# Gated mix of cached attention and a GEGLU FFN, decode: products of 20 of 128 rows in PSUM, FFN weights loaded ahead of the last values, w_down's products spread over the last tile

## Chip, cores and metric

The kernel runs on one core of one Trainium2 chip. The metric is device time in microseconds of one execution, the median over runs. Besides, one execution was recorded by the hardware profiler; everything that is said of engines and queues comes from that recording.

## What is computed

One decode step for a batch of four: attention of 32 heads over a cache of 4096 keys and values, a GEGLU FFN on the same input, and a gate between them.

```python
# B=4, D=512, H=32, Sk=4096, Dh=128, F=1792, all float32
q = (x @ wq).reshape(B, 1, H, Dh).transpose(0, 2, 1, 3)
scores = einsum("bhqd,bhkd->bhqk", q, k_cache) * Dh**-0.5
p = softmax(scores)
a = einsum("bhqk,bhkd->bhqd", p, v_cache)          # -> (B, 1, H*Dh)
a = a @ wo
b = (gelu(x @ w_gate) * (x @ w_up)) @ w_down
g = sigmoid((x * gate_w).sum(-1))
out = g * a + (1 - g) * b
```

Keys and values are 268 MB each; everything else is 28 MB.

## The kernel before

The attention runs over 32 tiles. Tile i is four heads (HT) of one batch row b; four tiles make a group g. A head's 4096 positions lie on 32 partitions with 128 rows (R) of 128 numbers each, so that a tile of keys is 128 partitions by 16384 floats, 8.39 MB, and one of values the same.

All large data passes through three buffers of that size (`kv`), used in turn: wq, k0, v0, k1, v1, and so on, and at the end f (w_gate and w_up), d (w_down and the first 18 rows of wo) and w (the last 14 rows of wo, in five pieces). Every load is issued on SyncE's queue, in this order; `load_next` issues the next one. A load waits until the last reader of its buffer is done: k(i+2) waits for the products of v(i), v(i+1) for the sum over k(i).

The order on each engine is as the program writes it. For one tile:

- VectorE multiplies the keys in place by the query (`multiply`, L188), sums over each row of 128 (`add_up`, L191) into SC, and finds a head's maximum (L200 to L204).
- ScalarE takes the exponentials into PM (`weights`, L207).
- TensorE multiplies PM with the values (`values`, L225, 32 products of two passes) into one of two PSUM banks PO[i % 2]; ScalarE copies that out (L228), TensorE gathers it into G (L231). Within iteration i this is done for tile i-1, after `multiply(i)` in program order.
- After a group, `totals` (L215) and `quotients` (L233 to L242) divide by the sums into OT, and `spread` (L173) lays out the next group's queries in QB by way of the bank QP.

In the last tile `multiply` and `add_up` go in pieces of 32 rows (CH), and ScalarE sums the first 32 rows (`add_up_beside`, L195).

Then comes the end: `totals`, `values` and `quotients` for the last tile; OT is spread over 128 partitions (L, L274; products L278) into OW (times the gate, L281) and OX (L284); FFN's up products (L294), gelu and gate (L296 to L306) into hT; 14 products with w_down and 18 with wo's first rows into one bank (L313); its copy a_sb (L315) starts the sum in acc (L318), wo's last 14 rows are added (L323), and the result is copied and stored (L326, L327).

Of the kernel before, what the change touches and what calls it, by code (L numbers as in the profile page):

```python
# [9 lines left out]
F32 = mybir.dt.float32  # L10
AF = mybir.ActivationFunctionType
OP = mybir.AluOpType
AX = mybir.AxisListType
# [4 lines left out]
def tile_gated_mix(ctx: ExitStack, tc: tile.TileContext, x, kc, vc, wq, wo, w_gate, w_up, w_down, gate_w, out):  # L18
    nc = tc.nc
    P = 128  # L20
    B, H, S, D = kc.shape
    DM = x.shape[2]
    F = w_gate.shape[1]
    KC = DM // P
    HT = 4
    PH = P // HT
    R = S // PH
    TW = R * D
    NG = H // HT
# [8 lines left out]
    CH = 32  # L38
    BASE = 24576
    scale = 1.0 / math.sqrt(D)  # L40
    c_gelu = math.sqrt(2.0 / math.pi)
# [9 lines left out]
    SC = front.tile([P, R], F32)  # L51
    RS = front.tile([P, B, HT], F32)
    QX = front.tile([P, B, HT, PH], F32)
# [3 lines left out]
    back = ctx.enter_context(tc.tile_pool(name="back", bufs=1))  # L57
# [3 lines left out]
    T = {}  # L61
# [10 lines left out]
    LOADS = []  # L72

    def load_kv(kind, i):
        nc.sync.dma_start(place((kind, i)), heads(kc if kind == "k" else vc, i))
# [17 lines left out]

    for i in range(NT):
        LOADS.append(lambda i=i: load_kv("k", i))
        LOADS.append(lambda i=i: load_kv("v", i))
    LOADS += [load_ffn_up, load_down, load_last]
    LOADS = iter(LOADS)

    def load_next():  # L100
        f = next(LOADS, None)
        if f:
            f()
# [23 lines left out]
    xT_ps = ps.tile([P, KC, B], F32, name="sm", bufs=2)  # L127
    for c in range(KC):
        nc.tensor.transpose(xT_ps[:, c, :], x_sb[:, c::KC], ident[:B, :B])  # L129
    for c in range(KC):  # L130
# [8 lines left out]
    z_ps = ps.tile([P, B], F32, name="sm", bufs=2)  # L139
# [5 lines left out]
    nc.vector.reciprocal(gates[:, 0], ez)  # L145
    nc.vector.tensor_scalar(gates[:, 1], gates[:, 0], -1.0, 1.0, op0=OP.mult, op1=OP.add)

    PO = [ps.tile([P, RJ * D], F32, name=f"po{s}") for s in range(2)]
    QP = ps.tile([P, B * D], F32, name="q")
    HG = H // 4  # L150
    HB = HG // 2
    w = T["q"].rearrange("p (c n) -> p c n", c=KC)
# [18 lines left out]
    QB = back.tile([P, B, D], F32)  # L171

    def spread(g):  # L173
        t = QP.rearrange("p (b d) -> p b d", b=B)
# [6 lines left out]
    dump = QX[:, 0].rearrange("p h k -> p (h k)")  # L181

    def keys(i):
        return T["k", i].rearrange("p (r d) -> p r d", d=D)

    def multiply(i, r0, r1):
        k = keys(i)[:, r0:r1]
        nc.vector.tensor_tensor(k, k, QB[:, i % B, None, :].to_broadcast([P, r1 - r0, D]), op=OP.mult)  # L188

    def add_up(i, r0, r1):  # L190
        nc.vector.tensor_reduce(SC[:, r0:r1], keys(i)[:, r0:r1], axis=AX.X, op=OP.add)  # L191

    def add_up_beside(i, r0, r1):
        for r in range(r0, r1):
            nc.scalar.activation(dump, keys(i)[:, r, :], AF.Copy, accum_out=SC[:, r:r + 1])  # L195

    def weights(i):
        b = i % B
# [12 lines left out]
    TOT = {}  # L211

    def totals(g):
        TOT[g] = ps.tile([P, B, HT], F32, name="sm", bufs=2)
        nc.tensor.matmul(TOT[g].rearrange("p b h -> p (b h)"), ones, RS.rearrange("p b h -> p (b h)"),  # L215
                         start=True, stop=True)

    def values(i):
        g, b = divmod(i, B)
        po = PO[i % 2]  # L220
        p = PM.rearrange("p r h -> p (r h)")
        n = R // RJ
        for j in range(n):
            c = j % 4
            nc.tensor.matmul(po[32 * c:32 * c + M], p[:, j * M:(j + 1) * M],  # L225
                             T["v", i][:, j * RJ * D:(j + 1) * RJ * D], start=j < 4, stop=j >= n - 4)
        o = back.tile([P, RJ * D], F32, name="o")
        nc.scalar.activation(o, po, AF.Copy)  # L228
# [4 lines left out]
    def quotients(g):  # L233
# [4 lines left out]
        t = ps.tile([P, B, HT], F32, name="sm", bufs=2)  # L238
# [3 lines left out]
        nc.vector.tensor_tensor(OT[:, :, HT * g:HT * g + HT], t, ri, op=OP.mult)  # L242

    spread(0)
    for i in range(NT):
        g, b = divmod(i, B)
        last = i == NT - 1
        multiply(i, 0, CH if last else R)
        if i > 0:
            if b == 0:  # L250
                totals(g - 1)
            values(i - 1)
            load_next()
        if b == 0 and i > 0:
            quotients(g - 1)
        if b == B - 1 and not last:
            spread(g + 1)
        if last:
            add_up_beside(i, 0, CH)
            for r in range(CH, R, CH):  # L260
                multiply(i, r, r + CH)
                add_up(i, r, r + CH)
        else:
            add_up(i, 0, R)
        weights(i)
        load_next()
    load_next()
    totals(NG - 1)
# [7 lines left out]
    t = ps.tile([P, B, 32], F32, name="sm", bufs=2)  # L276
# [9 lines left out]
    f = T["f"]  # L286
    spare = f[:, 2 * KC * F:2 * KC * F + 4 * FG].rearrange("p (a n) -> p a n", n=FG)
    u0, u1, t1, t2 = (spare[:, a, :] for a in range(4))
    for s, u in enumerate((u0, u1)):
        up = PO[s][:, :FG]  # L290
        for c in range(KC):
            for j in range(4):
                n0 = (s * KC + c) * F + j * FG
                nc.tensor.matmul(up[32 * j:32 * j + 32], xT[:, c, :], f[:, n0:n0 + FG],  # L294
                                 start=c == 0, stop=c == KC - 1)
        nc.scalar.activation(u, up, AF.Copy)  # L296
    nc.vector.tensor_tensor(t1, u0, u0, op=OP.mult)
    nc.vector.tensor_scalar(t1, t1, 0.044715, 1.0, op0=OP.mult, op1=OP.add)
    nc.vector.tensor_tensor(t1, t1, u0, op=OP.mult)
    nc.scalar.activation(t2, t1, AF.Tanh, scale=c_gelu)  # L300
    nc.vector.scalar_tensor_tensor(t1, t2, 1.0, u0, op0=OP.add, op1=OP.mult)
    nc.vector.scalar_tensor_tensor(t2, t1, 0.5, u1, op0=OP.mult, op1=OP.mult)
    hs = u0.rearrange("p (i r) -> p i r", i=DR)
    nc.vector.transpose(hs, t2.rearrange("p (q i) -> p i q", i=DR))
    hT = back.tile([P, DR, B], F32, name="hT")
    nc.vector.tensor_tensor(hT, hs[:, :, ::8], gates[:, 1, None, :].to_broadcast([P, DR, B]), op=OP.mult)  # L306

    a = QP
    early = [(hT[:, i, :], T["d"][:, i * DM:(i + 1) * DM]) for i in range(DR)]
    early += [(OW[:, :, i], T["d"][:, (DR + i) * DM:(DR + i + 1) * DM]) for i in range(W1)]  # L310
    for n, (l, r) in enumerate(early):
        c = n % 4
        nc.tensor.matmul(a[32 * c:32 * c + B], l, r, start=n < 4, stop=n >= len(early) - 4)  # L313
# [3 lines left out]
    for c in range(4):  # L317
        nc.tensor.matmul(acc[32 * c:32 * c + 32], pick_b.rearrange("p b k -> p (b k)"),  # L318
                         a_sb[:, c * P:(c + 1) * P], start=True, stop=False)
    for i in range(W1, WR):  # L320
        for c in range(4):
            r0 = (i - W1) * DM + c * P
            nc.tensor.matmul(acc[32 * c:32 * c + 32], OX[:, i - W1].rearrange("p b k -> p (b k)"),  # L323
                             T["w"][:, r0:r0 + P], start=False, stop=i == WR - 1)
    res = back.tile([P, P], F32, name="res")
    nc.vector.tensor_copy(res, acc)  # L326
    nc.sync.dma_start(out.rearrange("b s (c n) -> c (b s) n", c=4), res[::8])  # L327
# [22 lines left out]
```

## Time and profile before

| | |
|---|---|
| median of 3 runs | 1337.32 us (1337.11 to 1337.6) |
| the profiled execution | 1336.9 us, span 1335.0 us |
| mean granted TensorE clock | 0.645 |
| VectorE busy | 1133.3 us, 85% |
| TensorE busy | 387.6 us, 29% |
| ScalarE busy | 119.8 us, 9% |
| read from HBM | 564.67 MB, 423 GB/s over the span |

A row of groups names line, engine, operation, the tiles written and read, the shape and the count; after the first bar stands the busy time and the mean of one in ns; after the second the idle time of the engine just before, and what ended it. A row of the timeline starts with its start and length in us. DMA issues on SyncE's queue are shown as SPq.

### The profile page before, as it was taken

The page shows a single profiled execution, that of the slowest core. Times are in us where ns is not written, and L with a number is a line of the kernel's source. Part 1 is how long each engine was busy: PE and PEld are TensorE (multiplying, and loading weights), DVE is VectorE, ACT ScalarE, POOL GpSimd, SP SyncE. Part 2 cuts the span into 40 slices and gives each one's busy share as a digit, 9 for nine tenths or more (in the row PEclk, how much of TensorE's full clock was granted, in tenths as well). Part 3 has the DMA queues.
Part 4 walks back from the last instruction along what each step waited for, and adds up shares of the span by engine and source line. Part 5 has one row for each costly group of instructions (what it writes and reads, how often), then busy time and mean ns, then how long its engine had stood idle before and what let it go on. Part 6 is the DMA issues. An engine that isn't in the chain of part 4 may idle for free.

```text
span 1335.0 us, 6193 instructions
## 1 busy us (share of the span) xinstructions
PE 387.6 (29%) x2590; PEld 100.4 (8%) x2590; DVE 1133.3 (85%) x221; ACT 119.8 (9%) x408; POOL 0.7 (0%) x6
## 2 busy tenths in 40 slices
PE   2133212333321333321233232122333212323237
PEld 0000000000000001000010000000010000100002
DVE  1788889888889988888998898998888889888851
ACT  0000010001100010000000010000100000000130
POOL 0000000000000000000000000000000000000000
PEclk9566556666556666655666665566666556666658
DMA  9999999999999999999999999999999999999995
GB/s 409 440 438 410 440 426 431 430 434 416 425 434 428 434 423 414 434 430 430 429 432 429 430 423 436 423 432 432 424 438 428 427 432 436 432 420 419 434 426 219
DMA packets 10719, 565.07 MB, mean 423 GB/s; under 512 B 1196, under 2 KB 1212, under 8 KB 1604
## 3 DMA queue, kind: packets, MB, share of 16 engines
q1 hardware_dynamic: 10692, 564.69, 98.6%
q8 instruction: 20, 0.33, 0.1%
q14 instruction: 7, 0.06, 0.0%
HBM read 564.67 MB, written 0.01 MB: 423 GB/s over the span
## 4 chain that ended last, share of the span: by engine, by line
DVE 44%; DMA 38%; PE 14%; ACT 3%; issue 1%; DVEq 0%; SPq 0%; ACTq 0%
DMA kv<-in_A_k_cache 38%; DVE SC L191 22%; DVE kv L188 21%; PE po L225 12%; ACT PM L207 3%; PE q L313 1%; PE po L294 1%; DVE m L200 0%; DVE mt L202 0%; DVE nm L204 0%; PE g L323 0%; DVE OT L242 0%; DVE ri L235 0%; ACT o L228 0%; PE g L231 0%
## 5 line engine op out<-in xcount | busy, mean ns | idle before, releaser
L188 DVE TENSOR_TENSOR kv<-kv,QB 128x16384 f32<-128x16384 f32 (+1 forms) x35 | 551.6, 15761 | 122.0 <-DMA kv<-in_A_k_cache 122.0
L191 DVE TENSOR_REDUCE SC<-kv 128x128 f32<-128x16384 f32 (+1 forms) x34 | 547.0, 16088 | 2.6
L225 PE MATMUL po<-kv,PM 128*16 128x512 f32 x2048 | 298.6, 749 | 668.2 <-ACT PM L207 668.2
L207 ACT ACTIVATE PM<-SC,nm 32x128 f32<-32x128 f32 x128 | 65.9, 515 | 775.6 <-DVE nm L204 772.9
L225 PEld LDWEIGHTS po<-kv,PM 128*16 128x16 f32 x2048 | 62.5, 114 | 890.1 <-ACT PM L207 683.2
L215 PE MATMUL sm<-RS,ones 128*128 128x16 f32 x16 | 4.9, 384 | 213.3 <-ACT PM L207 213.3
L228 ACT ACTIVATE o<-po 128x512 f32<-128x512 f32 x32 | 19.1, 597 | 309.0 <-PE po L225 309.0
L231 PE MATMUL g<-o,wide 128*64 128x512 f32 x64 | 34.3, 618 | 25.1 <-ACT o L228 25.1
L207 ACT ACTIVATION_READ_ACCUMULATOR PM<-SC,nm 32x1 f32 x128 | 24.9, 195 | 0.0
L215 PEld LDWEIGHTS sm<-RS,ones 128*128 128x128 f32 x16 | 4.0, 311 | 215.6 <-ACT PM L207 215.6
L131 DVE COPY xT<-sm 128x32 f32<-128x32 f32 x4 | 0.5, 184 | 21.3 <-PE sm L129 21.3
L242 DVE TENSOR_TENSOR OT<-sm,ri 128x16 f32<-128x16 f32 x8 | 1.4, 175 | 13.5 <-PE sm L241 12.8
L326 DVE COPY res<-g 128x128 f32<-128x128 f32 x1 | 0.3, 290 | 14.1 <-PE g L323 14.1
L231 PEld LDWEIGHTS g<-o,wide 128*64 128x64 f32 x64 | 6.1, 134 | 54.5 <-ACT o L228 54.5
L200 DVE TENSOR_REDUCE m<-SC 128x1 f32<-128x128 f32 x32 | 9.2, 286 | 1.2
L241 PE MATMUL sm<-ident,gs 64*128 64x16 f32 x64 | 8.5, 262 | 5.4 <-ACT gs L237 5.4
L195 ACT ACTIVATE QX<-kv 128x128 f32<-128x128 f32 x32 | 9.9, 309 | 1.0
L179 ACT ACTIVATE QB<-q 128x512 f32<-128x512 f32 x8 | 4.8, 597 | 56.9 <-DVE kv L188 55.2
L178 PE MATMUL q<-ident,QX 128*128 128x128 f32 x64 | 9.2, 287 | 0.6 <-DVE QT L167 0.6
L167 DVE COPY QT<-q 128x16 f32<-128x16 f32 x8 | 0.9, 180 | 9.3 <-PE q L165 9.3
L157 PE MATMUL po<-kv,xT 128*32 128x512 f32 x64 | 8.7, 705 | 0.0
L241 PEld LDWEIGHTS sm<-ident,gs 64*128 64x128 f32 x64 | 7.7, 187 | 12.5 <-ACT gs L237 12.5
(62 smaller groups left out, 94.4 us busy)
## 6 DMA issues: line engine op xcount, KB each, us to landing
kv<-in_A_wo SPq DMA_DIRECT2D x1, 4608.0 KB, 24.6
kv<-in_B_w_gate SPq DMA_DIRECT2D x1, 3584.0 KB, 20.4
kv<-in_B_w_up SPq DMA_DIRECT2D x1, 3584.0 KB
kv<-in_B_w_down SPq DMA_DIRECT2D x1, 3584.0 KB, 13.7
kv<-in_A_wo SPq DMA_DIRECT2D x2, 1024.0 KB, 15.0
kv<-in_A_wo SPq DMA_DIRECT2D x1, 768.0 KB
kv<-in_A_k_cache SPq DMA_DIRECT2D x32, 31.2
kv<-in_A_v_cache SPq DMA_DIRECT2D x32, 24.2
```

What stands on the lines that cost most here:

```text
L178: nc.tensor.matmul(t[:, b, :], QX[:, b].rearrange("p h k -> p (h k)"), ident, start=True, stop=True)
L188: nc.vector.tensor_tensor(k, k, QB[:, i % B, None, :].to_broadcast([P, r1 - r0, D]), op=OP.mult)
L191: nc.vector.tensor_reduce(SC[:, r0:r1], keys(i)[:, r0:r1], axis=AX.X, op=OP.add)
L195: nc.scalar.activation(dump, keys(i)[:, r, :], AF.Copy, accum_out=SC[:, r:r + 1])
L200: nc.vector.tensor_reduce(m1, SC, axis=AX.X, op=OP.max)
L207: nc.scalar.activation(PM[s, :, h], SC[s, :], AF.Exp, bias=nm[s, :], scale=1.0, accum_out=RS[s, b, h:h + 1])
L225: nc.tensor.matmul(po[32 * c:32 * c + M], p[:, j * M:(j + 1) * M], T["v", i][:, j * RJ * D:(j + 1) * RJ * D], start=j < 4, stop=j >= n - 4)
L228: nc.scalar.activation(o, po, AF.Copy)
L231: nc.tensor.matmul(G[g], wide[:, (3 - b) * M:(7 - b) * M], o, start=b == 0, stop=b == B - 1)
L241: nc.tensor.matmul(t, gs[:, j, :], pick[:, :, j, :], start=j == 0, stop=j == RJ - 1)
L294: nc.tensor.matmul(up[32 * j:32 * j + 32], xT[:, c, :], f[:, n0:n0 + FG], start=c == 0, stop=c == KC - 1)
L313: nc.tensor.matmul(a[32 * c:32 * c + B], l, r, start=n < 4, stop=n >= len(early) - 4)
```

## The change

Three things, with what they need:

- **20 rows of products in PSUM.** `multiply` writes the products of the last 20 of a tile's 128 rows to a PSUM tile `big` (five of the eight banks), and those of the other 108 in place as before. `add_up` sums the 108 rows first, then the 20 from PSUM. The load that follows is asked for before `weights` instead of after it. To make room, PO's two banks become one (`po`), QP lies in `big` during the first projection and in `po` later, and the small results share one bank `sm`. The last tile is treated like the others: no pieces, nothing summed by ScalarE.
- **f is loaded before v31**, in the buffer of k30; v31 then has that of v30, d that of k31 and w that of f. FFN's up products stand in the last iteration after `gather(30)`, gelu after the loop.
- **w_down's 14 products** stand in groups of 4, 4 and 6 behind the last values, inside `quotients` and before L's products (`project`); wo's first 18 rows follow after OX. In acc the first four of wo's last rows come first, then a_sb's four products, then the other ten rows.

```diff
-    LOADS += [load_ffn_up, load_down, load_last]
+        if i == NT - 1:
+            LOADS.append(load_ffn_up)
         LOADS.append(lambda i=i: load_kv("v", i))
+    LOADS += [load_down, load_last]
...
+    RP = 20
+    R1 = R - RP
...
+    big = ps.tile([P, RP, D], F32, name="big")
+    flat = big.rearrange("p r d -> p (r d)")
+    po = ps.tile([P, RJ * D], F32, name="po")
+    sm = ps.tile([P, 4 * P], F32, name="sm")
...
-    PO = [ps.tile([P, RJ * D], F32, name=f"po{s}") for s in range(2)]
-    QP = ps.tile([P, B * D], F32, name="q")
+    PO = [po, flat[:, :RJ * D]]
+    QP = flat[:, RJ * D:2 * RJ * D]
...
+    def multiply(i):
+        k = keys(i)
+        q = QB[:, i % B, None, :]
+        nc.vector.tensor_tensor(big, k[:, R1:], q.to_broadcast([P, RP, D]), op=OP.mult)
+        nc.vector.tensor_tensor(k[:, :R1], k[:, :R1], q.to_broadcast([P, R1, D]), op=OP.mult)
+
+    def add_up(i):
+        nc.vector.tensor_reduce(SC[:, :R1], keys(i)[:, :R1], axis=AX.X, op=OP.add)
+        nc.vector.tensor_reduce(SC[:, R1:], big, axis=AX.X, op=OP.add)
...
+        if i == NT - 1:
+            ffn_up()
+        add_up(i)
+        load_next()
         weights(i)
-        load_next()
     load_next()
+    hT = gelu()
...
+    def project(count):
+        for _ in range(count):
+            n, (kind, r) = next(todo)
+            l = hT[:, r, :] if kind == "h" else OW[:, :, r]
+            r0 = (r if kind == "h" else DR + r) * DM
+            c = n % 4
+            nc.tensor.matmul(a[32 * c:32 * c + B], l, down[:, r0:r0 + DM], start=n < 4, stop=n >= len(order) - 4)
+
     totals(NG - 1)
     values(NT - 1)
-    load_next()
-    quotients(NG - 1)
+    project(4)
+    gather(NT - 1)
+    quotients(NG - 1, lambda: project(4))
...
+    project(DR - 8)
...
+    project(W1)
...
     for i in range(W1, WR):
+        if i == W1 + PIECES[0]:
+            for c in range(4):
+                nc.tensor.matmul(acc[32 * c:32 * c + 32], pick_b.rearrange("p b k -> p (b k)"),
+                                 a_sb[:, c * P:(c + 1) * P], start=False, stop=False)
         for c in range(4):
             r0 = (i - W1) * DM + c * P
             nc.tensor.matmul(acc[32 * c:32 * c + 32], OX[:, i - W1].rearrange("p b k -> p (b k)"),
-                             T["w"][:, r0:r0 + P], start=False, stop=i == WR - 1)
+                             T["w"][:, r0:r0 + P], start=i == W1, stop=i == WR - 1)
```

`ffn_up` and `gelu` hold the lines that stood at L286 to L306, but FFN's two halves use `po` one after the other; `gather` holds what stood at L227 to L231; `quotients` calls its second argument between the copy of G and its four products.

More of the change, by code (lines that the diff above doesn't have):

```diff
@@ L37, in tile_gated_mix @@
     PIECES = (4, 4, 3, 2, 1)
-    CH = 32
+    RP = 20
+    R1 = R - RP
     BASE = 24576
@@ L125, in tile_gated_mix @@
     nc.vector.tensor_copy(pick_b, wide[:, 3 * M:3 * M + B, None].to_broadcast([P, B, 8]))
-    xT_ps = ps.tile([P, KC, B], F32, name="sm", bufs=2)
+    big = ps.tile([P, RP, D], F32, name="big")
+    flat = big.rearrange("p r d -> p (r d)")
+    po = ps.tile([P, RJ * D], F32, name="po")
+    sm = ps.tile([P, 4 * P], F32, name="sm")
+    xT_ps = sm[:, :KC * B].rearrange("p (c b) -> p c b", c=KC)
     for c in range(KC):
@@ L138, in tile_gated_mix @@
     nc.vector.tensor_tensor(zd, ident[:B, :B], z.to_broadcast([B, B]), op=OP.mult)
-    z_ps = ps.tile([P, B], F32, name="sm", bufs=2)
+    z_ps = sm[:, 32:32 + B]
     nc.tensor.matmul(z_ps, ones[:B, :], zd, start=True, stop=True)
@@ L173, in spread @@
     def spread(g):
-        t = QP.rearrange("p (b d) -> p b d", b=B)
+        t = po.rearrange("p (b d) -> p b d", b=B)
         for b in range(B):
@@ L179, in spread @@
         nc.scalar.activation(QB, t, AF.Copy, scale=scale)
-    dump = QX[:, 0].rearrange("p h k -> p (h k)")
     def keys(i):
         return T["k", i].rearrange("p (r d) -> p r d", d=D)
[L186 to L195, printed above, removed]
+    def multiply(i):
[6 more added lines that the diff above has]
+        nc.vector.tensor_reduce(SC[:, R1:], big, axis=AX.X, op=OP.add)
     def weights(i):
@@ L213, in totals @@
     def totals(g):
-        TOT[g] = ps.tile([P, B, HT], F32, name="sm", bufs=2)
-        nc.tensor.matmul(TOT[g].rearrange("p b h -> p (b h)"), ones, RS.rearrange("p b h -> p (b h)"),
-                         start=True, stop=True)
+        TOT[g] = sm[:, 64:64 + B * HT].rearrange("p (b h) -> p b h", b=B)
+        nc.tensor.matmul(sm[:, 64:64 + B * HT], ones, RS.rearrange("p b h -> p (b h)"), start=True, stop=True)
     def values(i):
-        g, b = divmod(i, B)
-        po = PO[i % 2]
         p = PM.rearrange("p r h -> p (r h)")
@@ L226, in values, with gather @@
                              T["v", i][:, j * RJ * D:(j + 1) * RJ * D], start=j < 4, stop=j >= n - 4)
+    def gather(i):
+        g, b = divmod(i, B)
         o = back.tile([P, RJ * D], F32, name="o")
@@ L231, in values, with quotients @@
         nc.tensor.matmul(G[g], wide[:, (3 - b) * M:(7 - b) * M], o, start=b == 0, stop=b == B - 1)
-    def quotients(g):
+    def quotients(g, between=lambda: None):
         ri = back.tile([P, B, HT], F32, name="ri")
@@ L237, in quotients @@
         nc.scalar.activation(gs.rearrange("p j d -> p (j d)"), G[g], AF.Copy)
-        t = ps.tile([P, B, HT], F32, name="sm", bufs=2)
+        between()
+        t = sm[:, 128:128 + B * HT].rearrange("p (b h) -> p b h", b=B)
         pick = ident[:B * M, :B * M].rearrange("p (b j h) -> p b j h", b=B, j=RJ)
@@ L242, in quotients, with ffn_up, gelu @@
         nc.vector.tensor_tensor(OT[:, :, HT * g:HT * g + HT], t, ri, op=OP.mult)
+    def ffn_up():
+        f = T["f"]
+        for s in range(2):
+            up = po[:, :FG]
+            for c in range(KC):
+                for j in range(4):
+                    n0 = (s * KC + c) * F + j * FG
+                    nc.tensor.matmul(up[32 * j:32 * j + 32], xT[:, c, :], f[:, n0:n0 + FG],
+                                     start=c == 0, stop=c == KC - 1)
+            nc.scalar.activation(f[:, 2 * KC * F + s * FG:2 * KC * F + (s + 1) * FG], up, AF.Copy)
+    def gelu():
+        f = T["f"]
+        spare = f[:, 2 * KC * F:2 * KC * F + 4 * FG].rearrange("p (a n) -> p a n", n=FG)
+        u0, u1, t1, t2 = (spare[:, a, :] for a in range(4))
+        nc.vector.tensor_tensor(t1, u0, u0, op=OP.mult)
+        nc.vector.tensor_scalar(t1, t1, 0.044715, 1.0, op0=OP.mult, op1=OP.add)
+        nc.vector.tensor_tensor(t1, t1, u0, op=OP.mult)
+        nc.scalar.activation(t2, t1, AF.Tanh, scale=c_gelu)
+        nc.vector.scalar_tensor_tensor(t1, t2, 1.0, u0, op0=OP.add, op1=OP.mult)
+        nc.vector.scalar_tensor_tensor(t2, t1, 0.5, u1, op0=OP.mult, op1=OP.mult)
+        hs = u0.rearrange("p (i r) -> p i r", i=DR)
+        nc.vector.transpose(hs, t2.rearrange("p (q i) -> p i q", i=DR))
+        hT = back.tile([P, DR, B], F32, name="hT")
+        nc.vector.tensor_tensor(hT, hs[:, :, ::8], gates[:, 1, None, :].to_broadcast([P, DR, B]), op=OP.mult)
+        return hT
     spread(0)
@@ L246, in tile_gated_mix @@
         g, b = divmod(i, B)
-        last = i == NT - 1
-        multiply(i, 0, CH if last else R)
+        multiply(i)
         if i > 0:
@@ L252, in tile_gated_mix @@
             values(i - 1)
+            gather(i - 1)
             load_next()
@@ L255, in tile_gated_mix @@
             quotients(g - 1)
-        if b == B - 1 and not last:
+        if b == B - 1 and i < NT - 1:
             spread(g + 1)
[L258 to L264, printed above, removed]
+        if i == NT - 1:
+            ffn_up()
+        add_up(i)
+        load_next()
         weights(i)
-        load_next()
     load_next()
+    hT = gelu()
+    a = flat[:, :DM]
+    down = T["d"]
+    order = [("h", n) for n in range(DR)] + [("o", n) for n in range(W1)]
+    todo = iter(enumerate(order))
+    def project(count):
[5 more added lines that the diff above has]
+            nc.tensor.matmul(a[32 * c:32 * c + B], l, down[:, r0:r0 + DM], start=n < 4, stop=n >= len(order) - 4)
     totals(NG - 1)
     values(NT - 1)
-    load_next()
-    quotients(NG - 1)
+    project(4)
+    gather(NT - 1)
+    quotients(NG - 1, lambda: project(4))
     L = back.tile([P, B * H, 4], F32, name="o")
@@ L275, in tile_gated_mix @@
                             pick_q[:, None, :].to_broadcast([P, B * H, 4]), op=OP.mult)
-    t = ps.tile([P, B, 32], F32, name="sm", bufs=2)
+    project(DR - 8)
+    t = sm[:, 256:256 + B * 32].rearrange("p (b i) -> p b i", b=B)
     for b in range(B):
@@ L284, in tile_gated_mix @@
         nc.vector.tensor_copy(OX[:, :, b], OW[:, b, W1:, None].to_broadcast([P, WR - W1, 8]))
[L286 to L313, printed above, removed]
+    project(W1)
     a_sb = back.tile([P, DM], F32, name="gs")
@@ L316, in tile_gated_mix @@
     acc = ps.tile([P, P], F32, name="g")
-    for c in range(4):
-        nc.tensor.matmul(acc[32 * c:32 * c + 32], pick_b.rearrange("p b k -> p (b k)"),
-                         a_sb[:, c * P:(c + 1) * P], start=True, stop=False)
     for i in range(W1, WR):
+        if i == W1 + PIECES[0]:
+            for c in range(4):
+                nc.tensor.matmul(acc[32 * c:32 * c + 32], pick_b.rearrange("p b k -> p (b k)"),
+                                 a_sb[:, c * P:(c + 1) * P], start=False, stop=False)
         for c in range(4):
```

## The prediction

> **What bounds the kernel now.** I read the page's shares and queues first, then the groups by form, then one tile of the timeline, then windows of the transfer rate, then the timeline of the end.
>
> ```profile
> span 1335.0 us, 6193 instructions
> q1 hardware_dynamic: 10692, 564.69, 98.6%
> L188 DVE TENSOR_TENSOR kv<-kv,QB 128x16384 f32<-128x16384 f32 x31 | 534.0, 17225 | 118.0 <-DMA kv<-in_A_k_cache 118.0
> L191 DVE TENSOR_REDUCE SC<-kv 128x128 f32<-128x16384 f32 x31 | 533.7, 17217 | 2.4
> ```
>
> The profiled execution took 1336.9 us, 1.9 more than its span; the median of the runs is 1337.32, 0.4 above it. The one queue keeps the 16 DMA engines busy 98.6% of the span. VectorE still idles 118.0/31 = 3.8 us per tile, waiting for keys. So the transfers set the pace, and only two things can be won: time in which the queue runs below its rate, and work left over after the last transfer. First, one tile:
>
> ```profile
> 434.52 17.23 DVE L188 TENSOR_TENSOR kv<-kv,QB 128x16384 f32<-128x16384 f32 x1 [3.29 <-DMA kv<-in_A_k_cache]
> 443.45 0.33 SPq L75 DMA_DIRECT2D kv<-in_A_k_cache  x1
> 451.85 17.22 DVE L191 TENSOR_REDUCE SC<-kv 128x128 f32<-128x16384 f32 x1
> 469.10 0.33 SPq L75 DMA_DIRECT2D kv<-in_A_v_cache  x1
> 469.67 0.19 DVE L204 TENSOR_REDUCE nm<-mt 128x1 f32<-128x32 f32 x1
> 474.41 17.23 DVE L188 TENSOR_TENSOR kv<-kv,QB 128x16384 f32<-128x16384 f32 x1 [4.55 <-DMA kv<-in_A_k_cache]
> ...
> 42.34 17.23 DVE L188 TENSOR_TENSOR kv<-kv,QB 128x16384 f32<-128x16384 f32 x1 [5.10 <-DMA kv<-in_A_k_cache]
> ...
> 1216.93 17.23 DVE L188 TENSOR_TENSOR kv<-kv,QB 128x16384 f32<-128x16384 f32 x1 [3.40 <-DMA kv<-in_A_k_cache]
> ```
>
> A tile takes (1216.93 - 42.34)/30 = 39.15 us. Its values (8.39 MB) are issued the moment L191 has read the key buffer out, 469.10, only 5.3 us before the keys ahead of them in the queue have landed (474.41). The next keys are issued at 443.45, 31 us before they land, which is more than half a transfer ahead of the landing before theirs. Windows over eight tiles (us, busy by engine, clock, DMA share, GB/s) show what that does; long windows lie between two values issues, short ones run from an issue to 2 us past the next L188:
>
> ```profile
> 357.80:390.30 32.50, 9.24 (x66) 2.52 (x54) 32.40 (x4) 1.19 (x2) 0.00 (x0) 0.66 1.00 432
> 390.30:397.90 7.60, 4.24 (x20) 0.83 (x24) 2.96 (x5) 2.06 (x8) 0.00 (x0) 0.50 0.99 423
> ...
> 436.50:469.00 32.50, 7.95 (x54) 1.56 (x46) 32.40 (x2) 0.60 (x1) 0.00 (x0) 0.66 1.01 438
> 469.00:476.40 7.40, 4.24 (x21) 0.83 (x25) 2.74 (x5) 2.07 (x8) 0.00 (x0) 0.50 0.90 363
> ...
> 632.90:665.40 32.50, 7.96 (x62) 2.40 (x54) 32.40 (x2) 2.10 (x6) 0.00 (x0) 0.66 1.01 438
> 665.40:671.90 6.50, 3.35 (x18) 1.16 (x22) 2.75 (x5) 2.07 (x8) 0.00 (x0) 0.50 0.93 393
> ...
> 370.30:376.80 6.50, 0.00 (x0) 0.00 (x0) 6.40 (x4) 0.00 (x0) 0.00 (x0) 0.55 0.95 413
> ...
> 645.40:651.90 6.50, 0.00 (x0) 0.00 (x0) 6.40 (x2) 0.60 (x1) 0.00 (x0) 0.50 1.05 454
> ```
>
> The eight long windows average 437.5 GB/s, the eight short ones 384. The last two rows are the first and last of eight windows over the other handover, values to keys, where the next transfer was issued much earlier: they average 431. So the queue loses time at the keys-to-values handover, where the next transfer arrives late, and hardly at the other.
>
> Then the end:
>
> ```profile
> 1251.51 0.33 SPq L75 DMA_DIRECT2D kv<-in_A_v_cache  x1
> 1256.26 4.42 DVE L188 TENSOR_TENSOR kv<-kv,QB 128x4096 f32<-128x4096 f32 x1 [3.99 <-DMA kv<-in_A_k_cache]
> 1287.55 0.42 SPq L85 DMA_DIRECT2D kv<-in_A_wo  x1
> 1290.77 9.60 PE L225 MATMUL po<-kv,PM 128*16 128x512 f32 x64
> 1300.44 2.24 SPq L91 DMA_DIRECT2D kv<-in_A_wo  x5
> 1306.05 7.92 PE L294 MATMUL po<-kv,xT 128*32 128x448 f32 x64
> 1317.81 5.85 PE L313 MATMUL q<-kv,hT 128*4 128x512 f32 x26 [3.85 <-DVE hT L306]
> 1323.50 4.03 PE L313 MATMUL q<-kv,ow 128*4 128x512 f32 x34
> 1328.56 3.24 PE L323 MATMUL g<-kv,o 128*32 128x128 f32 x112
> 1331.87 0.29 DVE L326 COPY res<-g 128x128 f32<-128x128 f32 x1 [14.11 <-PE g L323]
> ...
> kv<-in_A_wo SPq DMA_DIRECT2D x1, 4608.0 KB, 24.6
> kv<-in_A_wo SPq DMA_DIRECT2D x1, 256.0 KB, 18.3
> ...
> 1256.20:1312.00 55.80, 27.58 (x194) 8.31 (x190) 33.78 (x19) 17.26 (x76) 0.00 (x0) 0.71 0.99 426
> ```
>
> The last piece of wo is issued at about 1302.3 (end of the five issues, 1302.7, less one) and lands 18.3 later, 1320.6. The queue is full until then (share 0.99). But PE only starts the w_down products at 1317.81, and the span ends 1335.0: 14.4 us after the last byte.
>
> **The change, part by part.**
>
> *Products in PSUM.* The same 32,768 element passes per tile, in four instructions instead of two. The slope of an element comes from the full rows and this one:
>
> ```profile
> L188 DVE TENSOR_TENSOR kv<-kv,QB 128x4096 f32<-128x4096 f32 x4 | 17.6, 4418 | 4.0 <-DMA kv<-in_A_k_cache 4.0
> L131 DVE COPY xT<-sm 128x32 f32<-128x32 f32 x4 | 0.5, 184 | 21.3 <-PE sm L129 21.3
> L326 DVE COPY res<-g 128x128 f32<-128x128 f32 x1 | 0.3, 290 | 14.1 <-PE g L323 14.1
> ```
>
> (17225 - 4418)/12288 = 1.042 ns an element and 0.15 us fixed. Reading PSUM: (290 - 184)/96 = 1.10 ns, the same within what two short rows tell. VectorE writing PSUM has no row; nearest is the SBUF row's 1.04 ns, and I bound it by that and twice that (2.08, 2.67 us more for 2,560 elements); below 1.04 I exclude, since no VectorE row here with two tensors is faster. I take 1.04. Two more instructions add 2 x (0.15 + 0.05 gap) = 0.4 us: VectorE's tile goes from 35.3 (434.52 to 469.86) to 35.7 us, still 3 us under the transfers' pace. What it buys: the key buffer is free after 2.82 + 14.56 + 14.56 + 0.15 = 32.1 us instead of 34.6, so the values are issued 2.5 us earlier. The reduction from PSUM comes after.
>
> What 2.5 us is worth: from below nothing (the handover costs the same wherever it falls; or less than nothing by the third rival); from above the whole dip, 39.15 - 16.78 MB/437.5 GB/s = 39.15 - 38.35 = 0.8 us a tile. Between them stands the fastest pair of tiles in the chain of waits:
>
> ```profile
> 827.09 17.23 DVE kv L188
> ...
> 904.58 17.24 DVE kv L188
> ```
>
> 77.49/2 = 38.75, a pace that the queue did hold. With 7.8 us instead of 5.3 ahead of the landing, the handover is near the other kind, so I take 0.37 us a tile, 30 x 0.37 = 11 us. By "DMA: Bandwidth & Descriptors" of the Trainium skill, section Where 436 GB/s comes from, the ceiling is 435.2 GB/s; an estimate from it is 38.55 us a tile and at most 18 us, beside the trace's 25 by the dip and 12 by the pair.
>
> *One bank `po` instead of two, `sm` as one bank.*
>
> ```profile
> 443.51 0.60 ACT L228 ACTIVATE o<-po 128x512 f32<-128x512 f32 x1 [10.04 <-PE po L225]
> ...
> 472.16 9.31 PE L225 MATMUL po<-kv,PM 128*16 128x512 f32 x64 [26.92 <-ACT PM L207]
> ```
>
> The next values' products start 28 us after the copy out of the last po, because they wait for PM; spread's use of po ends with QB, soon after the 17 us of L188. Nothing waits on the one bank. Cost 0; without that cover it would be the copy, 0.6 us, with the 3 us of slack behind it.
>
> *CH gone.* In the last tile ScalarE had summed 32 rows; now VectorE does all: 35.7 instead of 31.9 us (1256.26 to 1288.0), so PM comes 3.9 us later, at about 1294.2, and the values' products start at 1294.8 instead of 1290.8.
>
> *FFN's weights ahead of the last values.* f (7.34 MB) is issued in the old place of v31, 1251.5, less 2.5; v31 after values(30), at 1263.6; both wait behind k31 in a full queue, so no gap. v31 lands 7.34 MB/0.43 = 17 us later than now, about 1256.3 + 17 + 19.4 = 1292.7: before PM. SP queues f, v31, down, last in order; down waits for the last key buffer, 1256.3 + 32.1 = 1288.4 (now 1287.2), 4 us before v31 ends; last takes f's buffer and waits for FFN's products and gelu, done by 1298, 13 us before the queue would run dry at 1311. So the last landing stays where it is, 1320.6. FFN's products (7.92 us) run at about 1266 to 1283, in PE's empty stretch; gelu's VectorE and ScalarE steps, which now fit between the first of FFN's products and the first of w_down's (11.8 us with 7.9 of products), run under the values' products.
>
> *w_down in the pauses.* Values end at 1304.4; the chain gather, quotients, L, OW takes what it takes now, from the end of the values at 1300.4 to L294's start at 1306.05 and 0.4 for OW beside it, 6.0 us, plus fourteen products that PE does between (two passes each, 0.12 us a pass by 4.03/34, 3.3 us, two thirds of it under the copies and VectorE's steps): OW at about 1311.5. wo's first 18 rows land at 1287.55 + 24.6 = 1312.2, now some 0.3 later: their 36 passes end at 1316.8, four rows of L323's kind (32 passes at 0.029, 0.9) at 1317.7, a_sb and its four products 0.4, ten rows as their pieces land, the last at 1320.6. End: 1320.6 + 0.3 (last row) + 3.1 (1331.87 to 1335.0) = 1324.0. That is 11 us less. This part lies between 0 and 11; if PE's clock were half there, as at 1317.81 (26 passes in 5.85), the 36 passes and the 112 would end some 6 us later.
>
> Sum: 1336.9 - 11 - 11 = 1314.9; plus 0.4 to the median, 1315.3. I say 1316.
>
> **The rivals.**
>
> *The loop does not gain* (price of the handover is not lateness): for it, nothing in the trace varies the lead by much within one kind of handover. Against it, 431 against 384. If PSUM writes cost twice, 2.67 us, the release comes at 34.8 and the gain is gone the same way, VectorE at 38.4 still just keeping pace. Time: 1337.3 - 11 = 1326. Whether PSUM traffic in place of SBUF traffic itself speeds the transfers is another matter: the long windows have VectorE at 32.4 of 32.5 us and the best rate, so no. "SBUF — State Buffer" of the Trainium skill, section Who interferes with whom, says DMA never contends with a compute engine; the trace agrees, 437.5 GB/s beside a full VectorE.
>
> *The end does not gain fully*: the last tile's chain is 4 us later and OW meets wo's landing within 1 us; with a slow clock on PE the end is chain-bound and loses 6 of the 11: 1322.
>
> *Slower: PSUM at half rate for both writing and reading.* 2 x 2.67 = 5.3 us on VectorE's 35.7 gives 41.1 us a tile, and VectorE becomes the bound: 31 x (41.1 - 39.15) = 60 us, the last chain 5 us later: 1337 + 60 - 6 = 1391. It decides from 3 us, that is 0.58 ns an element over 1.04 both ways. Against it the reading slope, 1.10; for it only that writing was never seen.
>
> **How the numbers follow.** Forecast 60%, loop without gain 15%, end short 8%, slower 13%, and 4% that both gains vanish (1335 to 1338). What can be told from no change is 0.2%, 2.7 us. Faster: 60 + 15 + 8 and a bit = 0.84; same 0.03; slower 0.13. Range: below, loop 14 and end 11 give 1312, with the dip's bound further down, so 1309; above it takes in the loop without gain, 1326, and an end a little short, 1329.
>
> **What would show it.** L188 and L191 in two forms each, the 20-row ones at 2.8 us; values issued 32.1 us after the tile's first product; the short windows near 430 GB/s; a tile at 38.75 us; the first L188 of the last tile near 1245; v31 landing before the last Exp; the last product less than 0.5 us after wo's last piece, and the span ending 3.5 us after it. It is wrong if a 20-row form takes over 4.2 us, if the tile stays at 39.15, or if PE reaches the last row after its landing.

## The result, and the profile after

The changed kernel takes 1316.34 us (median of 4 runs, 1315.85 to 1316.96) against 1337.26 us before (4 runs, 1337.11 to 1337.6): a ratio of 0.9843, 95% interval 0.9826 to 0.9861. The profiled execution took 1315.85 us with a span of 1314.1, 20.9 less than before.

The page's span and queue, and the groups of the loop with shapes kept apart (tiles 0 to 30):

```profile
span 1314.1 us, 6186 instructions
...
q1 hardware_dynamic: 10692, 564.69, 99.5%
...
L195 DVE TENSOR_TENSOR kv<-kv,QB 128x13824 f32<-128x13824 f32 x31 | 451.1, 14551 | 0.0
L198 DVE TENSOR_REDUCE SC<-kv 128x108 f32<-128x13824 f32 x31 | 451.1, 14550 | 2.4
...
L194 DVE TENSOR_TENSOR big<-kv,QB 128x2560 f32<-128x2560 f32 x31 | 87.8, 2833 | 87.9 <-DMA kv<-in_A_k_cache 87.9
L199 DVE TENSOR_REDUCE SC<-big 128x20 f32<-128x2560 f32 x31 | 87.2, 2814 | 0.0
```

VectorE writes 2,560 products to PSUM in 2.833 us and sums them from PSUM in 2.814. In SBUF, by the slope of before (1.042 ns an element) and its 4,096-element form, 2,560 products would take 4.418 - 1,536 x 0.001042 = 2.82 us. So PSUM costs what SBUF costs, to within 0.02 us.

The timeline of one tile, as shown for before:

```profile
42.26 2.83 DVE L194 TENSOR_TENSOR big<-kv,QB 128x2560 f32<-128x2560 f32 x1 [3.28 <-DMA kv<-in_A_k_cache]
...
430.40 2.83 DVE L194 TENSOR_TENSOR big<-kv,QB 128x2560 f32<-128x2560 f32 x1 [3.12 <-DMA kv<-in_A_k_cache]
...
462.27 2.81 DVE L199 TENSOR_REDUCE SC<-big 128x20 f32<-128x2560 f32 x1
462.38 0.33 SPq L76 DMA_DIRECT2D kv<-in_A_v_cache  x1
...
469.38 2.83 DVE L194 TENSOR_TENSOR big<-kv,QB 128x2560 f32<-128x2560 f32 x1 [3.51 <-DMA kv<-in_A_k_cache]
...
1244.89 2.83 DVE L194 TENSOR_TENSOR big<-kv,QB 128x2560 f32<-128x2560 f32 x1 [3.21 <-DMA kv<-in_A_k_cache]
```

The values are issued at 462.38, while the sum from PSUM still runs, 32.0 us after the tile's first product (before: 34.6) and 7.0 us ahead of the next tile. From the first tile's start to the last one's a tile takes (1244.89 - 42.26)/31 = 38.79 us; over the same 31 steps it was (1256.26 - 42.34)/31 = 39.16. That is 11.3 us. The rest of the span, from the last tile's start, went from 78.7 to 69.2 us: 9.5 us.

The same windows as before, from a values issue to 2 us past the next tile's start, and from there to the next issue (us, busy by engine, clock, DMA share, GB/s; first, an inner and the last pair of eight, and between them the slowest short one):

```profile
386.80:393.80 7.00, 1.16 (x8) 0.32 (x12) 5.41 (x6) 2.08 (x8) 0.00 (x0) 0.50 1.03 440
393.80:423.80 30.00, 9.02 (x62) 1.77 (x54) 29.90 (x4) 0.60 (x1) 0.00 (x0) 0.67 1.00 435
...
462.40:471.40 9.00, 3.23 (x16) 0.66 (x20) 5.39 (x5) 2.06 (x8) 0.00 (x0) 0.50 0.99 430
471.40:501.40 30.00, 7.83 (x62) 2.40 (x54) 29.90 (x4) 2.10 (x6) 0.00 (x0) 0.67 1.01 435
...
542.40:548.80 6.40, 0.58 (x4) 0.15 (x8) 5.41 (x5) 2.08 (x8) 0.00 (x0) 0.50 0.93 389
...
656.10:665.10 9.00, 3.19 (x18) 1.10 (x22) 5.43 (x5) 2.06 (x8) 0.00 (x0) 0.50 1.03 444
665.10:697.20 32.10, 9.32 (x66) 3.27 (x58) 30.06 (x6) 1.19 (x2) 0.00 (x0) 0.66 1.00 431
```

The eight handovers now average 432 GB/s and the stretches between them 433: the dip to 384 is gone. Over all 27 handovers between the third tile and the 30th, the same windows give 398 before and 433 now, and the stretches between 435 and 433. So the eight windows of before were among its slower ones, and the stretches between did not stay at 437. One short window, at 542, still has 389. It belongs to the first tile of a group, where the timeline shows something new:

```profile
508.26 2.83 DVE L194 TENSOR_TENSOR big<-kv,QB 128x2560 f32<-128x2560 f32 x1 [3.41 <-DMA kv<-in_A_k_cache]
...
525.47 0.25 DVE L239 RECIPROCAL ri<-sm 128x16 f32<-128x16 f32 x1
...
525.86 1.86 PE L246 MATMUL sm<-ident,gs 64*128 64x16 f32 x8 [6.71 <-DVE ri L239]
527.76 0.17 DVE L247 TENSOR_TENSOR OT<-sm,ri 128x16 f32<-128x16 f32 x1 [2.04 <-PE sm L246]
...
542.42 0.33 SPq L76 DMA_DIRECT2D kv<-in_A_v_cache  x1
```

`totals` and `quotients` now write one bank. PE's products L246 wait 6.7 us until VectorE has read the totals (L239), which VectorE does only behind the multiplication; then VectorE waits 2.04 us for L246 before it may sum. In such a tile the values are issued 34.2 us after the first product. In the loop's seven such tiles VectorE idles 14.3 us before L247 and PE 48.3 us before L246; before, PE did these products right after the copy of G. (The page's 24.7 us for L247 holds another 10.4 us at the end of the kernel, where VectorE already idled 12.8 us before.)

Then the end:

```profile
1262.77 5.40 PE L256 MATMUL po<-kv,xT 128*32 128x448 f32 x32 [5.18 <-DMA kv<-in_B_w_up]
...
1283.21 9.27 PE L226 MATMUL po<-kv,PM 128*16 128x512 f32 x64
...
1285.88 2.23 SPq L92 DMA_DIRECT2D kv<-in_A_wo  x5
...
1301.39 5.69 PE L309 MATMUL big<-kv,ow 128*4 128x512 f32 x34 [2.27 <-DMA kv<-in_A_wo]
...
1308.52 2.37 PE L342 MATMUL g<-kv,o 128*32 128x128 f32 x80
1310.95 0.29 DVE L345 COPY res<-g 128x128 f32<-128x128 f32 x1 [10.87 <-PE g L342]
...
kv<-in_A_wo SPq DMA_DIRECT2D x1, 256.0 KB, 22.2
```

FFN's products are done at 1268, in PE's empty stretch. The last piece of wo is issued at about 1287.7 and lands 22.2 us later, 1309.9; PE ends 1.0 us after that (1308.52 + 2.37 = 1310.9), where before it ended 11 us after.

### The profile page after: what moved, and what is told of

The parts are those of the page before. It is cut to its first block, busy times and chain, and to the rows that moved or that the text cites. A ratio compares the mean times of both kernels' runs of the same rounds, so it can differ in the third digit from the quotient of the medians.

```text
span 1314.1 us, 6186 instructions
## 1 busy us (share of the span) xinstructions
PE 390.0 (30%) x2590; PEld 106.1 (8%) x2590; DVE 1141.1 (87%) x280; ACT 107.0 (8%) x344; POOL 0.7 (0%) x6
## 4 chain that ended last, share of the span: by engine, by line
DVE 41%; DMA 41%; PE 12%; ACT 3%; issue 2%; SPq 0%; DVEq 0%; ACTq 0%
DMA kv<-in_A_k_cache 38%; DVE SC L198 18%; DVE kv L195 18%; PE po L226 11%; DVE SC L199 3%; ACT PM L211 2%; DMA kv<-in_A_wo 2%; DVE big L194 2%; DMA o<-in_A_x 2%; PE big L309 0%; PE po L164 0%; PE big L164 0%; DVE m L204 0%; PE sm L219 0%; PE g L342 0%
## 5 line engine op out<-in xcount | busy, mean ns | idle before, releaser
L226 PE MATMUL po<-kv,PM 128*16 128x512 f32 x2048 | 294.0, 739 | 613.4 <-ACT PM L211 613.4
L198 DVE TENSOR_REDUCE SC<-kv 128x108 f32<-128x13824 f32 x32 | 465.6, 14550 | 2.5
L195 DVE TENSOR_TENSOR kv<-kv,QB 128x13824 f32<-128x13824 f32 x32 | 465.6, 14551 | 0.0
L194 DVE TENSOR_TENSOR big<-kv,QB 128x2560 f32<-128x2560 f32 x32 | 90.6, 2833 | 91.2 <-DMA kv<-in_A_k_cache 91.2
L199 DVE TENSOR_REDUCE SC<-big 128x20 f32<-128x2560 f32 x32 | 90.1, 2814 | 0.0
L246 PE MATMUL sm<-ident,gs 64*128 64x16 f32 x64 | 14.1, 356 | 48.3 <-DVE ri L239 48.3
L247 DVE TENSOR_TENSOR OT<-sm,ri 128x16 f32<-128x16 f32 x8 | 1.4, 174 | 24.7 <-PE sm L246 24.7
L246 PEld LDWEIGHTS sm<-ident,gs 64*128 64x128 f32 x64 | 13.4, 308 | 55.1 <-issue 54.3
L256 PE MATMUL po<-kv,xT 128*32 128x448 f32 x64 | 8.6, 692 | 5.3 <-DMA kv<-in_B_w_up 5.2
L185 PE MATMUL po<-ident,QX 128*128 128x128 f32 x64 | 9.2, 286 | 0.0
```

Source lines behind the costliest of these rows:

```text
L194: nc.vector.tensor_tensor(big, k[:, R1:], q.to_broadcast([P, RP, D]), op=OP.mult)
L195: nc.vector.tensor_tensor(k[:, :R1], k[:, :R1], q.to_broadcast([P, R1, D]), op=OP.mult)
L198: nc.vector.tensor_reduce(SC[:, :R1], keys(i)[:, :R1], axis=AX.X, op=OP.add)
L199: nc.vector.tensor_reduce(SC[:, R1:], big, axis=AX.X, op=OP.add)
```

## Experiments

Medians in us; the ratio is to runs of the kernel before on the same chip. A tile is the mean of 31 steps between the first and the last tile's start, the end is the span less the last tile's start, both from the one profiled execution of each.

| kernel | median (runs) | ratio, 95% interval | tile | end |
|---|---|---|---|---|
| before | 1337.26 (4) | | 39.16 | 78.7 |
| changed | 1316.34 (4) | 0.9843, 0.9826 to 0.9861 | 38.79 | 69.2 |
| e1_psum_sum_first | 1337.85 (8) | 1.0029, 1.0014 to 1.0044 | 39.26 | 71.9 |
| e2_loop_alone | 1325.52 (3) | 0.9906, 0.9854 to 0.9958 | 38.84 | 78.0 |
| e3_all_in_place | 1337.56 (8) | 1.0003, 0.9984 to 1.0022 | 39.39 | 72.2 |
| e4_8_rows | 1328.65 (4) | 0.9945, 0.9912 to 0.9979 | 39.14 | 70.5 |
| e9_in_place_recip_first | 1325.92 (2) | 0.9915, 0.9887 to 0.9942 | 39.09 | 70.8 |
| e5_reciprocal_first | 1314.34 (4) | 0.9830, 0.9812 to 0.9848 | 38.76 | 68.4 |
| e6_six_after_L | 1315.57 (4) | 0.9838, 0.9821 to 0.9855 | 38.83 | 68.1 |
| e10_three | 1314.29 (4) | 0.9828, 0.9807 to 0.9848 | 38.77 | 68.4 |
| e7_no_pauses | 1315.20 (2) | 0.9856, 0.9837 to 0.9876 | 38.77 | 69.4 |
| e8_before_sum_108 | 1321.71 (2) | 0.9905, 0.9885 to 0.9925 | 38.78 | 75.5 |
| e11_8_rows_recip_first | 1315.98 (4) | 0.9864, 0.9848 to 0.9881 | 38.77 | 70.2 |
| e12_sum_first_recip_first | 1327.66 (4) | 0.9952, 0.9934 to 0.9971 | 39.11 | 70.8 |

The kernel before itself spread from 1331.7 to 1342.3 us on the chip of e1 to e4, so their medians alone say less than their ratios and traces. The runs were on several chips, and the median of before differs between them: 1335.9 with e1 to e4, 1337.0 with e5, e6, e9 and e10, 1334.7 with e7, e8, e11 and e12.

**Loop and end apart.** e2 is the kernel before with the 20 rows in PSUM, and its own order of loads and end.

```diff
-        multiply(i, 0, CH if last else R)
+        if last:
+            multiply(i, 0, CH)
+        else:
+            multiply_both(i)
...
-            add_up(i, 0, R)
+            add_up_both(i)
```

> The kernel before with only the 20 rows in PSUM (tiles 0 to 30, with one po bank and one sm bank); its order of loads, its last tile in pieces and its end are those of before. Theory (two separate gains, loop 11.4 us and end 9.5 us): 1337.3 - 11.4 = about 1326. Rival (the loop's gain needs the new order at the end, or the end's gain feeds on the loop): above 1330 or below 1322.

It came out at 1325.5, with a tile of 38.84 us and the old end of 78.0: the two gains are separate, and the loop's is what was expected. This rests on its trace; the interval of the ratio is wide, 5.6 to 19.5 us of gain.

**Is it the time of the issue?** e1 swaps the two sums, e3 puts all products back into the key buffer, e4 takes 8 rows.

```diff
     def add_up(i):
-        nc.vector.tensor_reduce(SC[:, :R1], keys(i)[:, :R1], axis=AX.X, op=OP.add)
         nc.vector.tensor_reduce(SC[:, R1:], big, axis=AX.X, op=OP.add)
+        nc.vector.tensor_reduce(SC[:, :R1], keys(i)[:, :R1], axis=AX.X, op=OP.add)
```

> The changed kernel with the two sums of a tile in the other order: the 20 rows in PSUM first, the 108 rows in the key buffer last, so that the key buffer is released at the end of the sums, some 34.9 us after the tile's first product instead of 32.0, and all work and all PSUM traffic stay. Theory (the loop gained because the values are issued earlier, ahead of the end of the keys' transfer): the tile goes back to about 39.2 us from 38.79, the time to 1316.3 + 30 x 0.4 = about 1328. Rival (less SBUF traffic of VectorE, or the four shorter instructions, made the transfers faster): the tile stays at 38.8 us and the time at 1316 to 1317.

> The changed kernel with all 128 rows of products in the key buffer again, one multiplication and one sum per tile; the new end, load order and banks stay. Theory: the tile is back at 39.15 us and the end keeps its gain, 1316.3 + 11.4 = about 1328. Rival (the transfers are faster for another part of the change, such as the order of issues): 1316 to 1319 with a tile of 38.8 us.

> The changed kernel with 8 instead of 20 rows in PSUM: the key buffer is free 1.1 us instead of 2.7 us before the end of the sums, that is about 33.7 us after the tile's first product instead of 32.0. Theory (what counts is how long before the end of the keys' transfer the values are issued, with most of the loss gone once that is over some 3 us): between the two ends and nearer to the changed kernel per row, about half of the loop's gain, 1320 to 1324, tile near 39.0 us. Rival (relief by PSUM traffic in proportion to the rows): 8/20 of 11.4 gained, 1323. Rival (PSUM without any effect on the loop): 1316.

All three lost the loop's gain, as the theory has it, but e1 and e3 were near 1338, some 10 us above the forecast, and e4 at 1328.7 was 5 above its range. The timeline of e3 shows why, in the first tile of a group:

```profile
516.28 17.23 DVE L194 TENSOR_TENSOR kv<-kv,QB 128x16384 f32<-128x16384 f32 x1 [3.73 <-DMA kv<-in_A_k_cache]
...
535.71 0.17 DVE L245 TENSOR_TENSOR OT<-sm,ri 128x16 f32<-128x16 f32 x1 [2.04 <-PE sm L244]
...
553.04 0.33 SPq L76 DMA_DIRECT2D kv<-in_A_v_cache  x1
...
555.76 17.22 DVE L194 TENSOR_TENSOR kv<-kv,QB 128x16384 f32<-128x16384 f32 x1 [1.96 <-DMA kv<-in_A_k_cache]
```

The wait on `sm` moves the values to 36.8 us after the first product, only 2.7 us ahead of the next tile. In these three it costs far more than in the changed kernel, where the values still have 4.5 us: the tile behind a group's first one takes 40.65 us in e3, 40.1 in e1 and 39.95 in e4 (means of seven), against 38.9 in the changed kernel. So the shared bank was mixed into all three. The next runs take it away.

**The wait on the shared bank.** e5 is the changed kernel with VectorE's reciprocals ahead of the next multiplication; e9 is e3 with the same.

```diff
+        if b == 0 and i > 0:
+            totals(g - 1)
+            reciprocals(g - 1)
         multiply(i)
         if i > 0:
-            if b == 0:
-                totals(g - 1)
             values(i - 1)
```

> The changed kernel with all 128 rows in the key buffer (as in e3_all_in_place) and with the reciprocals of a group ahead of the next tile's multiplication instead of behind it, so that no product has to wait for VectorE on the shared bank sm. e3 came out at 1337.6, 9 us above what was expected; its trace shows the values of every group's first tile issued 2.2 us later than in the other tiles. Theory (that new wait on sm, made late by one bank for two results, costs e3 its loop: 39.39 instead of 39.16 us a tile): all values are issued 34.6 us after the tile's first product, the tile is back at 39.15 and the time at 1329 to 1331. Rival (e3 is slow for another reason, such as the new order at the end): 1335 to 1338 again.

> The changed kernel with the reciprocals of a group ahead of the next tile's multiplication. Theory (the lead of the values' issue sets the loss): the values of a group's first tile are issued 32.0 us after its first product instead of 34.2, VectorE's 24.7 us of idling before L247 go, and the time falls by 1 to 2.5 us, to about 1314.5. Rival (at 32.0 as at 34.2 the lead is long enough): no difference that can be told, 1316.

e9 fell to 1325.9, 3 us below its range, though its ratio's interval reaches up to 1329: nothing but this wait was between e3 and the end's gain alone. Its tile of 39.09 us also shows that all the rest of the change, without the 20 rows in PSUM, gives the loop 0.07 us a tile. e5 came to 1314.3, as expected, though its interval overlaps with that of the changed kernel; what the wait did is plain in the trace. Of the 24.7 us of idling that were expected to go, the loop's 14.3 were this wait. Timeline of e5, first tile of a group:

```profile
506.79 0.26 DVE L241 RECIPROCAL ri<-sm 128x16 f32<-128x16 f32 x1 [2.95 <-PE sm L219]
507.17 2.83 DVE L194 TENSOR_TENSOR big<-kv,QB 128x2560 f32<-128x2560 f32 x1
...
518.34 1.06 PE L251 MATMUL sm<-ident,gs 64*128 64x16 f32 x8 [0.68 <-ACT gs L246]
...
524.38 0.17 DVE L252 TENSOR_TENSOR OT<-sm,ri 128x16 f32<-128x16 f32 x1
...
539.15 0.33 SPq L76 DMA_DIRECT2D kv<-in_A_v_cache  x1
```

The reciprocals stand in VectorE's pause for keys, the products are done 5 us before VectorE asks for them, and the values are issued 32.0 us after the first product in this tile too.

**The same question again, without that wait.** e12 is e5 with the two sums swapped as in e1; e11 is e5 with `RP = 8` (the PSUM tile keeps its five banks).

> The kernel of e5_reciprocal_first with the 20 PSUM rows summed first, so that all PSUM traffic stays and the key buffer is released at the end of the sums, 34.5 us after the first product in every tile. Theory (only the time of the issue counts): as e9, all in place, 1325 to 1327. Rival (PSUM traffic in place of SBUF traffic has a share in the gain): 1315 to 1322.

> The kernel of e5_reciprocal_first (1314.3) with 8 rows in PSUM instead of 20: values issued 33.6 us after every tile's first product. Theory (the loss is gone once the values come some 3 us ahead of the first engine's end of the keys; e4 fell short because of its groups' first tiles at 35.8): most of the gain, 1316 to 1318. Rival (gain in proportion to the rows): 8/20 of the 11.6 us between e9 (1325.9) and e5, about 1321.

e12 went to 1327.7, just above its range, and a tile of 39.11 us; e11, on the same chip, stayed at 1316.0 and 38.77. e12 differs from e5 in the order of two instructions and nothing else: same work, same PSUM traffic, values issued at 34.5 instead of 32.0. Its windows, first and last pair of seven:

```profile
389.60:396.30 6.70, 3.63 (x20) 0.83 (x24) 2.68 (x4) 2.07 (x8) 0.00 (x0) 0.50 0.98 411
396.30:428.80 32.50, 6.96 (x50) 1.33 (x42) 32.49 (x4) 0.60 (x1) 0.00 (x0) 0.66 1.01 438
...
623.70:629.80 6.10, 3.00 (x16) 0.66 (x20) 2.66 (x5) 2.07 (x8) 0.00 (x0) 0.50 0.95 399
629.80:662.40 32.60, 7.67 (x62) 2.35 (x54) 32.57 (x5) 2.10 (x6) 0.00 (x0) 0.71 0.99 429
```

The dip is back, 409 on average at the handover and 435 between. And e11's one microsecond of earlier issue was worth as much in the loop as e5's 2.5, so the gain is not in proportion to the lead. At a pace of 38.7 us an issue at 34.5 would come 4.2 us ahead of the keys' landing, and it loses; one at 33.6 comes 5.1 ahead and loses almost nothing. Later than that the loss grows, as the tiles of e4, e1 and e3 behind a group's first one show (issues at 35.8 to 36.9). By its ratio e11 falls 4.5 us short of e5, on another chip; the traces show 1.8 us of it in the end (70.2 against 68.4) and next to nothing in the loop, and the rest stays open. Relief by PSUM traffic is out.

**Without PSUM.** e8 is the kernel before with shorter sums: it leaves the last 20 of a tile's rows out of them, so their scores stay 0 and it computes something else.

```diff
+    nc.vector.memset(SC, 0.0)
...
-            add_up(i, 0, R)
+            add_up(i, 0, R - 20)
```

> The kernel before, without PSUM for products, whose sums leave out the last 20 of a tile's 128 rows in tiles 0 to 30 (their scores stay 0): the key buffer is released 2.7 us earlier and VectorE has 2.7 us less to do per tile; everything else is as before. Theory (the earlier issue is what the loop gains by, wherever the rows go): tile at 38.75 to 38.8 us, time 1337.3 - 11.5 = 1326, as e2_loop_alone. Rival (the gain needs products in PSUM): 1335 to 1337.

The tile is 38.78 us: an earlier release is enough, wherever the rows go. VectorE has 2.7 us less to do per tile here; e11 and e12 do without that. The time, 1321.7, is 4 below the forecast, mainly because the end took 75.5 instead of 78.7 us. Of these 3.2 us, 2.7 are PE's clock, told below.

**The end.** e6 moves six of w_down's products behind L's, e7 puts all 14 behind OX, e10 has e5, e6 and wo's first rows in two loads.

```diff
-    project(DR - 8)
     t = sm[:, 256:256 + B * 32].rearrange("p (b i) -> p b i", b=B)
     for b in range(B):
         nc.tensor.matmul(t[:, b, :], ...)
+    project(DR - 8)
```

> The changed kernel with the last six of w_down's 14 products behind L's four products instead of ahead of them, where PE now idles 2.3 us before wo's rows have landed. Theory (the 36 passes with wo's first rows ran 5.7 us at a lower clock because of that pause, so that PE reaches the last row late): they take about 4.2 us, the last product ends 0.3 instead of 0.9 us after wo's last piece, and the time falls by 0.5 to 1 us, to about 1315.6. Rival (the end is bound by the landing alone): 1316.3.

> The changed kernel with w_down's 14 products in one block behind OX, together with wo's first 18, instead of in the pauses of the last tile; FFN's weights and products stay early. Theory (the pauses save PE 28 passes behind OW, 3.4 to 4.7 us, of which PE has some 2.3 us of waiting to give): 1318 to 1320, 2 to 4 us above the changed kernel, so that most of the end's 9.5 us come from FFN's early products. Rival (the pauses are what counts): 1323 or more. Rival (the end is bound by wo's landing alone): 1316.

> Both of these (reciprocals first, six products behind L's) and wo's first 18 rows loaded in two pieces of nine, so that PE can begin with them while the second lands. Theory: the gains add, 2 + 0.8 us: 1313 to 1314. Rival (the transfers' own pace is reached): as e5_reciprocal_first, 1314.5.

Timeline of PE, first two rows of e6, then two of e7:

```profile
1301.85 4.04 PE L309 MATMUL big<-kv,ow 128*4 128x512 f32 x34 [1.46 <-DMA kv<-in_A_wo]
...
1309.76 1.06 PE L342 MATMUL g<-kv,o 128*32 128x128 f32 x24 [0.42 <-DMA kv<-in_A_wo]
```

```profile
1297.50 5.61 PE L309 MATMUL big<-kv,hT 128*4 128x512 f32 x26
...
1302.95 4.03 PE L309 MATMUL big<-kv,ow 128*4 128x512 f32 x34
```

In e6 the 34 passes take 4.04 instead of 5.69 us, at a granted clock of 1.00 instead of 0.67, and PE waits for wo's last pieces (0.42 us): the end is bound by the landing, 68.1 us. The 0.8 us that it gains are as expected, but inside the intervals. e7 is the surprise: without any pauses it is at 1315.2, no slower than the changed kernel. Its 26 passes with w_down start at 1297.50, when the changed kernel's PE would soon wait for wo, and the block ends at about the same time (1302.95 + 4.03 = 1307.0 against 1307.5). So the pauses were worth nothing that these runs can tell. The end's 9.5 us come from the rest: FFN's early weights and products, together with the new order in acc, which no run here takes apart. e10 is as e5, 1314.3: the gains did not add. Its 34 passes took 5.39 us again, but PE ends only about 0.5 us behind the last landing, as in e5, so little but the transfers' own pace is left. e5 and e10 are below both kernels.

## Why the prediction was right, point by point

- *The queue sets the pace, and the handover from keys to values loses time because the values come late.* Shown, by e12 against e5, and against e11 on its own chip. What was wrong is the number beside it: I set 7.8 against 5.3 us ahead of the landing, but the 5.3 had the loss of its tile in it (39.9 us long). It is 6.7 against 4.1 at full pace; 4.2 loses, and 5.1 loses almost nothing.
- *0.37 us a tile, 11 us.* Measured 11.3 (39.16 to 38.79). That the fastest pair of tiles in the trace of before, 38.75, gave the size was in part luck: e5's mean is 38.76, but its fastest pair runs at 38.55 and two of its tiles take 40.2. The bound from the dip's windows, 0.8 us, was twice too high, because the eight windows were slower than the rest (384 against 398) and the stretches between did not keep 437 GB/s.
- *VectorE to PSUM costs 1.04 ns an element.* It does: 2.83 us for 2,560. The slower rival fell with that.
- *One bank po, one bank sm: nothing waits.* For po right. For sm this step failed: the prediction looked at po alone and gave sm the same answer. The order "products after reciprocals" goes into PE as a wait, and the reciprocals stand behind 17 us of multiplication. It held VectorE 2 us in each group's first tile. The medians differ by 2.0 us (e5), with overlapping intervals; the traces put 1.1 us of that in the loop. With 20 rows of early release there was room for it; without (e3 against e9) it cost 11.6.
- *The last landing stays, and PE is there before it.* The landing stayed within 0.7 us relative to the last tile (65.0 against 64.3 us after its start). PE was late by 0.7 us more than predicted, because after 2.27 us of waiting for wo, 34 passes took 5.69 us instead of 4, at a clock of 0.67. They end 62.6 us after the last tile's start, where the sum had 60.5. So PE reached the last row after its landing, which was one of the signs of being wrong: this step of the end failed. It is the rival "the end does not gain fully", at about a tenth of its price. End 9.5 instead of 11.
- *w_down in the pauses.* Counted as part of the 11 us; e7 shows that it brings nothing, since PE has to wait for wo anyhow.
- The sum: 11.3 + 9.5 against 11 + 11, 1316.3 against 1316. That they meet so closely is luck: the sum gave 1315.3, and rounding it up to 1316 made room for about half of what the end fell short.
- *What can be told from no change is 0.2%.* Too small: runs of the kernel before spread over 10.6 us on one chip.

## What to carry to other kernels

When a queue is busy nearly all the time, look at its rate in windows around each handover before calling it saturated: a transfer that is issued only a few microseconds before the queue would run dry cost 0.4 us on average here, and releasing a buffer one microsecond sooner won all of it. Where results share a bank, a wait goes into the engine that writes next; put the reader of the first result into a pause of its engine ahead of a long instruction. Work whose inputs can be loaded early should be moved under the transfers as a whole before it is cut into pauses.

## Not expected of the hardware

A late transfer costs rate while the queue still looks nearly full: in the kernel before, the eight windows at the handover have a DMA share of 0.90 to 0.99, so the engines were mostly busy but moved 384 instead of 437 GB/s. What they do in that time isn't shown by any run here.

TensorE's clock after one and the same pause differs between runs. In both the kernel before and e8 PE waits 3.85 us for hT and then starts the products with w_down. Windows over that pause and over the products, first before, then e8 (clock is the third number from the end):

```profile
1313.90:1317.80 3.90, 0.06 (x4) 0.00 (x0) 2.45 (x4) 1.12 (x2) 0.00 (x0) 0.82 1.02 429
1317.80:1323.50 5.70, 5.69 (x29) 1.01 (x33) 0.00 (x0) 0.00 (x0) 0.00 (x0) 0.52 0.25 99
```

```profile
1301.30:1305.10 3.80, 0.01 (x2) 0.00 (x0) 2.44 (x4) 1.12 (x2) 0.00 (x0) 1.00 1.01 421
1305.10:1308.20 3.10, 3.04 (x32) 0.79 (x36) 0.00 (x1) 0.00 (x0) 0.00 (x0) 1.00 0.54 215
```

In the first the clock fell to half in the pause and the first 26 passes took 5.85 us; in the second it stayed at 1.00 and they took 3.17. "TensorE: Matmul & The Clock Gate" of the Trainium skill, Part 1: The HAM clock gate, has the gate close after an idle window of about 3.4 us, and the window runs freely. That one pause has two outcomes agrees with a free-running window. But the first trace has the clock at 1.00 until 1316.4 and at half from there, about 2.5 us into the pause (0.82 is the mean over it), so there the gate did not wait for 3.4 us of idling within the pause. A pause of this length before the last stage makes its time a matter of luck, by 2.7 us here.
